# Attention and a gated layer on one core: more buffers for weight conversion, and loads and low parts moved in the order

## The chip, the cores and the metric

The kernel runs on one core of one Trainium2 chip. The metric is the device time of one launch in microseconds (us). The kernel before takes 1325.12 us, the median of three runs (1322.34 to 1326.35).

## The reference

```python
def _attn_ref(q, k, v):                       # 8 batches, 12 heads, 448 positions, head size 64
    S = q.shape[2]
    scores = q @ k.transpose(0, 1, 3, 2) / np.sqrt(q.shape[-1]) - np.log(S)
    return (1.0 / (1.0 + np.exp(-scores))) @ v          # a sigmoid in place of the softmax

def _moe_ref(x, w_gate, w_val, w_out):        # x 3584x768, w_gate and w_val 768x1536, w_out 1536x768
    gate = 1.0 / (1.0 + np.exp(-(x @ w_gate)))
    return gate * (x @ w_val) @ w_out
```

q, k and v come as float32. The attention's result, its heads side by side, is the x of the second part. The weights come as float64 and are read as pairs of 32-bit words. In the second part each operand is used as a high part and a low part, and three matmuls (low by high, high by low, high by high) make up one product.

## The kernel before

**Attention** (0 to about 279 us). The heads are taken in 24 groups of four ("quads", m = 0 to 23), three quads to a batch, and each quad in seven steps ("beats", g = 0 to 6). One beat has eight matmuls of `scores` (L254), a sigmoid on ScalarE (L266), and, two beats behind, the eight of `values` (L269). When a pair of heads is done, ScalarE copies one half of its sum out of PSUM and VectorE adds the other (`x<-av`, L297); the sum goes to DRAM (`xd`). There is one PSUM tile for each of the four sums of a quad, so TensorE can begin a sum of the next quad only when the add of the last one has been made, four beats earlier in the order.

**Conversion.** Beside this, VectorE and GpSimd turn the weights from float64 words into high and low parts. They come in chunks of 128x384. `Words.first` loads a chunk's next and does four VectorE operations (L109 to L112) on tiles `wa` and `wt`; `Words.second` does three more (L122 to L124), and `finish_lo` makes the low part (L128). `convert` (L130) is a generator that yields after each step. Each group of weights (one of six index pairs `jp`) has 32 steps. For each of two halves `t` there are four chunks of the gate or value weights, two steps each, with a cast and an add on GpSimd (L154, L157), and then four sums or differences of these chunks, one step each: an add and a cast on GpSimd (L167, L168) and the low part on VectorE (L170). These are the operands of a product with seven multiplications in place of eight. Then come four chunks of the output weights, two steps each, whose parts are sent to DRAM from `wa` and `wt` themselves (`od<-wt`, `od<-wa`, L139). The other results leave from tiles `whl` (three buffers) as `ad<-whl`. The first three groups (set 0) are converted in the attention at a fixed number of steps per beat, the other three (set 1) in the first visits of the second part, one step per 2.46 "ticks".

**x of the first batches.** From quad 8 on, `load_x` (L193) reads x of the first pair of batches back with 12 transfers, and `split_x` (L200), a generator too, makes of it seven operands of three tiles each in 21 steps: on GpSimd a difference (L209) and the cast to the high part (L213), on VectorE the low part (L215). One step is taken in beats 1, 3 and 5 of each quad from quad 9.

**The second part** has eight visits: set 0 with each of four pairs of batches (visits 0 to 3), then set 1 (visits 4 to 7). A visit has six units (gate and value, for each of three slots), and a unit has seven products of nine matmuls (`product`, L376), into four PSUM tiles `un`. ScalarE takes the first two products out of PSUM, VectorE the other five, in the order of the program, and GpSimd adds two of the partial sums (`u`, `c`, L393). A function in the list `later` is run after the matmuls of the next product. Each product also loads the operand that is seven ahead (`A<-ad`, L227); its transfer waits until TensorE has used the place. In a value unit, `value(i, acc)` multiplies gate and value (L438; VectorE for i = 0 and 2, GpSimd for 1 and 3), and `split` (L440) casts the result to its high part on ScalarE and takes the low part on VectorE.

Then come twelve output tiles of 18 matmuls each (L460). The first two take the first two slots before the last one. Eight places (`wo`) hold output weights: of the 18 loads of a visit eight have been made when its tiles begin, and three follow after every second tile (`load_out`, L231). In set 0 a tile is copied and stored as a partial sum (`part<-ob`). In set 1 the partial sum comes back (`pb<-part`, L466, two buffers), VectorE adds it (`plus`, L511), and the result is stored (`y<-ob`, two buffers of `ob`). Between the units and the tiles, x of the next visit is loaded, and its 21 split steps are taken two to a tile.

All transfers are issued by SyncE, in the order of the program. Each issue of the second part is also built to wait until the transfer eight issues before it has landed. VectorE, ScalarE and GpSimd run in the program's order too.

## Time and profile before

The profiled execution took 1328.51 us, of which the span from first to last instruction is 1326.7 us. It lies 3.4 us above the median of the runs.

| | TensorE | weight load | VectorE | ScalarE | GpSimd |
|---|---|---|---|---|---|
| busy, us | 1253.1 | 1029.1 | 757.0 | 440.4 | 483.2 |
| share of the span | 94% | 78% | 57% | 33% | 36% |

The granted TensorE clock was 0.983 on average. Transfers kept 78.5% of the 16 DMA engines' time, at 257 GB/s. In the rows, PE is TensorE, DVE VectorE, ACT ScalarE, POOL GpSimd and SPq the queue that issues transfers. A window's row gives its bounds and length in us, then each engine's busy time with the number of instructions, then the granted clock, the share of the DMA engines and GB/s. A row of waits gives the engine and line that waited, what it waited for, the us in total, the number of times and the longest. A row of the timeline gives start, length, instruction and, in brackets, the idle time before it with what ended it.

### The profile page before, as it was taken

The numbers are of one execution on the slowest core, as the hardware profiler recorded it, in microseconds if no ns is written. First come the engines' busy times: TensorE is split into PE (matmuls) and PEld (weight loads), VectorE is DVE, ScalarE is ACT, GpSimd is POOL, SyncE is SP. The second block draws the span as 40 slices with busy tenths as digits, with TensorE's granted clock in tenths as the row PEclk, the third lists the DMA queues.
The fourth block names the chain that finished last, engine by engine and source line by source line (L and its number), as shares of the span: only waits on it lengthen the run. The fifth ranks groups of instructions, "written<-read, shape, count | busy, mean of one in ns | idle before, by whom it ended". The sixth has DMA issues, their size and how long they took to land.

```text
span 1326.7 us, 20773 instructions
## 1 busy us (share of the span) xinstructions
PE 1253.1 (94%) x7456; PEld 1029.1 (78%) x7456; DVE 757.0 (57%) x1274; ACT 440.4 (33%) x700; POOL 483.2 (36%) x457
## 2 busy tenths in 40 slices
PE   9998789989998799978999899998999899989998
PEld 3443335768997799967899789997999799979998
DVE  6787888727757676645878645334434434443431
ACT  6776567732223122311242123222222312231210
POOL 3415824205563245612566233234123403241220
PEclk9999999999999899988999999999999999999999
DMA  8999688988978689676978876777777787778745
GB/s 316 319 349 326 241 274 311 317 281 253 312 263 303 200 271 334 218 278 198 308 271 294 281 241 214 217 216 251 242 216 213 232 263 217 230 227 269 215 128 178
DMA packets 159558, 341.12 MB, mean 257 GB/s; under 512 B 16352, under 2 KB 71776, under 8 KB 159456
## 3 DMA queue, kind: packets, MB, share of 16 engines
q1 hardware_dynamic: 159456, 339.80, 78.5%
q8 instruction: 59, 0.97, 0.3%
q14 instruction: 43, 0.35, 0.1%
HBM read 264.24 MB, written 75.50 MB: 256 GB/s over the span
## 4 chain that ended last, share of the span: by engine, by line
PE 61%; DVE 14%; DMA 11%; POOL 5%; issue 4%; SPq 2%; ACT 2%; DVEq 0%; POOLq 0%; ACTq 0%
PE un L385 34%; PE acc L460 14%; PE av L280 7%; PE sc L263 7%; DMA od<-wa 4%; DVE bl L215 2%; DMA wo<-od 2%; DVE c L393 1%; DMA ad<-whl 1%; DMA pb<-part 1%; DMA c<-xd 1%; POOL g L438 1%; DVE wa L109 1%; DVE wa L110 1%; DVE wt L122 1%
## 5 line engine op out<-in xcount | busy, mean ns | idle before, releaser
L385 PE MATMUL un<-bh,A 128*128 128x448 f32 x2016 | 590.1, 372 | 36.5 <-DVE c L393 19.3
L385 PEld LDWEIGHTS un<-bh,A 128*128 128x128 f32 x2016 | 385.2, 191 | 79.0 <-DVE c L393 23.8
L385 PE MATMUL un<-bl,A 128*128 128x448 f32 x1008 | 373.7, 371 | 0.0
L460 PE MATMUL acc<-hh,wo 128*128 128x448 f32 x1152 | 334.1, 369 | 15.0 <-DMA wo<-od 13.9
L460 PEld LDWEIGHTS acc<-hh,wo 128*128 128x128 f32 x1152 | 218.1, 189 | 36.9 <-DMA wo<-od 16.5
L280 PE MATMUL av<-a,v 64*64 64x448 f32 x1344 | 211.3, 540 | 16.0 <-DVE x L297 13.3
L460 PE MATMUL acc<-hl,wo 128*128 128x448 f32 x576 | 212.3, 369 | 0.5 <-DVE hl L442 0.4
L263 PE MATMUL sc<-qk 64*64 64x448 f32 x1344 | 211.0, 542 | 0.4 <-ACT a L266 0.4
L385 PEld LDWEIGHTS un<-bl,A 128*128 128x128 f32 x1008 | 192.5, 191 | 16.0
L266 ACT ACTIVATE a<-sc,bias 128x896 f32<-128x896 f32 x168 | 169.2, 1008 | 87.0 <-PE sc L263 77.2
L393 POOL TENSOR_TENSOR u<-u,p 128x448 f32<-128x448 f32 x48 | 56.1, 1169 | 388.8 <-DVE u L393 388.7
L441 ACT CAST hh<-g 128x448 fp32r<-128x448 f32 x96 | 52.8, 566 | 299.7 <-DVE g L438 232.0
L280 PEld LDWEIGHTS av<-a,v 64*64 64x64 f32 x1344 | 73.6, 134 | 78.8 <-issue 45.8
L263 PEld LDWEIGHTS sc<-qk 64*64 64x64 f32 x1344 | 73.1, 134 | 70.0 <-issue 52.2
L460 PEld LDWEIGHTS acc<-hl,wo 128*128 128x128 f32 x576 | 109.1, 189 | 10.4 <-DVE hl L442 1.4
L427 ACT ACTIVATE g<-c 128x448 f32<-128x448 f32 x96 | 51.6, 573 | 194.6 <-DVE c L393 191.8
L393 DVE TENSOR_TENSOR ob<-acc,pb 128x448 f32<-128x448 f32 x48 | 29.8, 622 | 121.4 <-DMA y<-ob 78.4
L442 DVE TENSOR_TENSOR hl<-g,hh 128x448 fp32r<-128x448 f32 x96 | 63.4, 663 | 62.0 <-ACT hh L441 61.4
L154 POOL CAST whl<-wt 128x384 fp32r<-128x384 f32 x48 | 37.5, 780 | 166.6 <-DVE wt L122 166.6
L438 POOL TENSOR_TENSOR g<-c,g 128x448 f32<-128x448 f32 x48 | 63.9, 1332 | 66.2 <-DVE c L393 63.6
L109 DVE TENSOR_SCALAR wa<-wraw 128x384 uint32<-128x384 uint32 x72 | 39.8, 552 | 80.2 <-DMA od<-wa 60.8
L393 DVE TENSOR_TENSOR c<-un,u 128x448 f32<-128x448 f32 x96 | 59.0, 618 | 31.2 <-PE un L385 29.8
(58 smaller groups left out, 1133.8 us busy)
## 6 DMA issues: line engine op xcount, KB each, us to landing
A<-ad SPq DMA_DIRECT2D x336, 384.0 KB, 3.9
wo<-od SPq DMA_DIRECT2D x144, 256.0 KB, 4.9
ad<-whl SPq DMA_DIRECT2D x84, 384.0 KB, 4.9
qk<-qk SPq DMA_DIRECT2D x23, 896.0 KB, 6.7
v<-vv SPq DMA_DIRECT2D x24, 448.0 KB, 6.3
xd<-x SPq DMA_DIRECT2D x48, 224.0 KB, 5.4
part<-ob SPq DMA_DIRECT2D x48, 224.0 KB, 4.2
pb<-part SPq DMA_DIRECT2D x48, 224.0 KB, 4.3
```

The source lines that it names most:

```text
L109: nc.vector.tensor_scalar(out=a, in0=raw[:, :, 1], scalar1=0x7FFFFFFF, scalar2=None, op0=ALU.bitwise_and)
L154: nc.gpsimd.tensor_copy(hl[:, 0], hi)
L263: nc.tensor.matmul(sc[halves[u], h, :S], lhsT=qkt[halves[h], p, k0:k0 + HP], rhs=qkt[halves[h], p, :S], start=True, stop=True)
L266: nc.scalar.activation(a, sc[:, :, :S], AF.Sigmoid, bias=bias, scale=scale)
L280: nc.tensor.matmul(avs[key][halves[h], :S], lhsT=vt[halves[u], g, h], rhs=a[halves[u], h], start=start, stop=g == last)
L385: nc.tensor.matmul(acc, lhsT=w, rhs=m, start=i == 0, stop=i == len(terms) - 1)
L393: engine.tensor_tensor(out=to, in0=x, in1=y, op=ALU.add)
L427: nc.scalar.activation(gates[i], acc, AF.Sigmoid)
L438: engine.tensor_tensor(out=g, in0=acc, in1=g, op=ALU.mult)
L441: nc.scalar.copy(hh, g)
L442: nc.vector.tensor_tensor(out=hl, in0=g, in1=hh, op=ALU.subtract)
L460: nc.tensor.matmul(acc, lhsT=w, rhs=m, start=i == 0 and some[0] == 0, stop=i == len(terms) - 1 and some[-1] == SET - 1)
```

## The change

- **Places.** In the attention `wa` and `wt` get four buffers in place of two and `whl` four in place of three. In the second part `wa` and `wt` get two in place of one; `whl` stays at three. `ob` gets three in place of two. A tile `wf4` is added, so that the second difference isn't written over the first sum.
- **Low parts of the sums** (`convert`). The VectorE operation of a sum, with its store, isn't issued at the start of the next step but goes to a list `unsplit`. There it waits until two sums stand behind it, or until a later step empties the list.
- **x of the first batches** is split in beats 1 and 5 of a quad, not 1, 3 and 5.
- **Low parts of the hidden values** (`value`). ScalarE's cast is issued at once where VectorE made the product and after the next product where GpSimd did. VectorE's low part follows one product behind the cast.
- **Loads.** The first two partial sums of a visit are loaded at its start, not between x and the tiles. `load_out` after every second tile stands ahead of that tile's add and of the next `pb` load.

```diff
@@ Words.first
-            a = self.pool.tile([P, CW], U32, tag="wa", name="wa")
-            t = self.pool.tile([P, CW], U32, tag="wt", name="wt")
+            a = self.pool.tile([P, CW], U32, tag="wa", name="wa", bufs=self.ahead)
+            t = self.pool.tile([P, CW], U32, tag="wt", name="wt", bufs=self.ahead)
@@ convert
+        def split(keep):
+            while len(unsplit) > keep:
+                to, hl, *where = unsplit.pop(0)
+                nc.vector.tensor_tensor(out=hl[:, 1], in0=to, in1=hl[:, 0], op=ALU.subtract)
+                store(hl, *where)
...
                     words.first()
+                    split(1)
                     send(1)
                     yield
                     send(0)
+                    split(0)
                     hi, a, e = words.second()
-                    hl = pool.tile([P, 2, CW], F32R, tag="whl", name="whl", bufs=3)
+                    hl = pool.tile([P, 2, CW], F32R, tag="whl", name="whl", bufs=words.held)
...
+                    split(1)
                     send(1)
-                    hl = pool.tile([P, 2, CW], F32R, tag="whl", name="whl", bufs=3)
+                    hl = pool.tile([P, 2, CW], F32R, tag="whl", name="whl", bufs=words.held)
                     nc.gpsimd.tensor_tensor(out=to, in0=x, in1=y, op=op)
                     nc.gpsimd.tensor_copy(hl[:, 0], to)
+                    unsplit.append((to, hl, jp, t, (1, 2, 3, 5)[n]))
                     yield
-                    nc.vector.tensor_tensor(out=hl[:, 1], in0=to, in1=hl[:, 0], op=ALU.subtract)
-                    store(hl, jp, t, (1, 2, 3, 5)[n])
@@
-        words = Words(att, chunks(sets[0]), AHEAD)
+        words = Words(att, chunks(sets[0]), AHEAD, 4)
...
-                if m > first_x and g % 2:
+                if m > first_x and g in (1, 5):
                     next(splits, None)
@@ value
-                def split():
+                def high():
                     nc.scalar.copy(hh, g)
-                    nc.vector.tensor_tensor(out=hl, in0=g, in1=hh, op=ALU.subtract)
-                if i == 2:
-                    split()
+                    later.append(lambda: nc.vector.tensor_tensor(out=hl, in0=g, in1=hh, op=ALU.subtract))
+                if engine is nc.vector:
+                    high()
                 else:
-                    later.append(split)
+                    later.append(high)
@@ visits
-        words = Words(ff, chunks(sets[1]), AHEAD_FF)
+        words = Words(ff, chunks(sets[1]), AHEAD_FF, 3)
...
             hs = []
+            if last_set:
+                load_part(pr, *tiles[0])
+                load_part(pr, *tiles[1])
...
                 load_x(nxt[1])
                 splits = split_x()
-            if last_set:
-                load_part(pr, *tiles[0])
-                load_part(pr, *tiles[1])
...
-                ob = ff.tile([P, S], F32, tag="ob", name="ob", bufs=2)
+                ob = ff.tile([P, S], F32, tag="ob", name="ob", bufs=3)
+                if t == 1:
+                    for _ in range(SET):
+                        load_out()
                 if s:
                     plus(ob, acc, pbs.pop((t, o)))
...
                 b = 2 * pr + t
-                if t == 1:
-                    for _ in range(SET):
-                        load_out()
```

How the order moves is shown at three places. In each the line numbers of the two kernels differ; the line of the same statement is 1 to 14 higher after, and L170 becomes L141.

SyncE between the units and the tiles of visit 5, before: the last load of x, three loads of partial sums, the first store, a fourth load, then the output weights.

```order
L197 DMA x_10463<-xd_5_94 128x448
L197 DMA x_10465<-xd_5_100 128x448
L466 DMA pb<-part_0_125 128x448
L466 DMA pb<-part_0_131 128x448
L466 DMA pb<-part_1_126 128x448
L522 DMA y<-ob 128x448
L466 DMA pb<-part_1_132 128x448
L235 DMA wo<-od_250 128x512
L235 DMA wo<-od_248 128x512
L235 DMA wo<-od_249 128x512
L522 DMA y<-ob 128x448
```

The same place after:

```order
L211 DMA x_10476<-xd_5_94 128x448
L211 DMA x_10478<-xd_5_100 128x448
L480 DMA pb<-part_1_126 128x448
L536 DMA y<-ob 128x448
L249 DMA wo<-od_250 128x512
L249 DMA wo<-od_248 128x512
L249 DMA wo<-od_249 128x512
L480 DMA pb<-part_1_132 128x448
L536 DMA y<-ob 128x448
```

The loads of `part_0_125` and `part_0_131` have gone to the visit's start, behind the last store of visit 4 and ahead of its first operand load. The three loads of output weights stand behind one load of a partial sum, not four.

VectorE in the last value unit of the last visit, before (L393 takes a product out of PSUM, L438 multiplies, L442 is the low part):

```order
L393 TENSOR_TENSOR c<-un,p_12375 128x448
L438 TENSOR_TENSOR g_12339<-c,g_12339 128x448
L442 TENSOR_TENSOR hl<-g_12339,hh 128x448
L393 TENSOR_TENSOR c<-un,u_12379 128x448
L442 TENSOR_TENSOR hl<-g_12354,hh 128x448
L442 TENSOR_TENSOR hl<-g_12357,hh 128x448
L393 TENSOR_TENSOR c<-un,u_12378 128x448
L438 TENSOR_TENSOR g_12373<-c,g_12373 128x448
L442 TENSOR_TENSOR hl<-g_12373,hh 128x448
```

The same after:

```order
L407 TENSOR_TENSOR c<-un,p_12391 128x448
L452 TENSOR_TENSOR g_12355<-c,g_12355 128x448
L456 TENSOR_TENSOR hl<-g_12355,hh 128x448
L407 TENSOR_TENSOR c<-un,u_12395 128x448
L407 TENSOR_TENSOR c<-un,u_12394 128x448
L452 TENSOR_TENSOR g_12389<-c,g_12389 128x448
L456 TENSOR_TENSOR hl<-g_12370,hh 128x448
L456 TENSOR_TENSOR hl<-g_12373,hh 128x448
L456 TENSOR_TENSOR hl<-g_12389,hh 128x448
```

The two low parts of what GpSimd multiplied have moved behind the last product's L407 and L452. ScalarE's and GpSimd's order in this place is unchanged.

VectorE in quads 9 and 10, where four sums are made (L170), x is split (L215) and the attention's sums are added (L297), before:

```order
L128 SCALAR_TENSOR_TENSOR whl<-wa,we 128x384
L215 TENSOR_TENSOR bl<-p_1298,bh 128x448
L170 TENSOR_TENSOR whl<-wf,whl 128x384
L297 TENSOR_TENSOR x<-av,x 128x448
L215 TENSOR_TENSOR bl<-u_1306,bh 128x448
L170 TENSOR_TENSOR whl<-wf,whl 128x384 x2
L297 TENSOR_TENSOR x<-av,x 128x448
L215 TENSOR_TENSOR bl<-g_1314,bh 128x448
L170 TENSOR_TENSOR whl<-wf,whl 128x384
L109 TENSOR_SCALAR wa<-wraw 128x384
```

The same after:

```order
L129 SCALAR_TENSOR_TENSOR whl<-wa,we 128x384
L311 TENSOR_TENSOR x<-av,x 128x448
L229 TENSOR_TENSOR bl<-p_1300,bh 128x448
L141 TENSOR_TENSOR whl<-wf,whl 128x384 x2
L311 TENSOR_TENSOR x<-av,x 128x448
L229 TENSOR_TENSOR bl<-u_1308,bh 128x448
L110 TENSOR_SCALAR wa<-wraw 128x384
L111 TENSOR_SCALAR wa<-wa 128x384
L112 TENSOR_SCALAR wt<-wa 128x384
L113 TENSOR_SCALAR wa<-wa 128x384
L141 TENSOR_TENSOR whl<-wf,whl 128x384 x2
```

The four low parts of the sums come later, the last two behind the first four operations of the next chunk, and two low parts of x stand where three stood.

13 lines of the change are left out of this document (9 added, 4 removed).

## The prediction

> **What bounds the kernel now.** I read the share of each engine on the page first, then busy times by stage, then in each slow stage what TensorE waits for, and then the queue behind that.
>
> ```profile
> PE 1253.1 (94%) x7456; PEld 1029.1 (78%) x7456; DVE 757.0 (57%) x1274; ACT 440.4 (33%) x700; POOL 483.2 (36%) x457
> ```
>
> TensorE is busy 94% of the span, so only what it loses can be won. The windows are cut where a stage's first matmul starts: the first nine quads; quads 9 to 16; then units and tiles of the visits.
>
> ```profile
> 4.46:98.80 94.34, 93.95 (x996) 38.04 (x992) 70.15 (x143) 69.91 (x80) 30.08 (x37) 1.00 0.96 335
> 98.80:203.30 104.50, 88.47 (x900) 35.96 (x896) 86.43 (x143) 62.76 (x72) 56.00 (x66) 0.98 0.80 279
> 279.30:365.20 85.90, 80.93 (x381) 72.78 (x380) 58.56 (x99) 17.96 (x35) 38.92 (x37) 0.96 0.87 287
> 365.20:409.50 44.30, 44.15 (x218) 40.48 (x217) 29.23 (x43) 17.13 (x34) 29.23 (x25) 1.00 0.77 266
> 409.50:504.00 94.50, 81.62 (x379) 72.97 (x378) 61.19 (x111) 17.27 (x34) 33.77 (x33) 0.95 0.81 260
> 548.50:647.50 99.00, 85.16 (x380) 75.24 (x379) 59.10 (x106) 19.25 (x38) 36.81 (x35) 0.91 0.73 245
> 692.40:775.00 82.60, 77.82 (x380) 70.70 (x380) 58.17 (x101) 18.54 (x36) 33.50 (x31) 1.00 0.85 280
> 775.00:821.80 46.80, 44.39 (x218) 40.50 (x217) 25.76 (x31) 17.29 (x34) 18.48 (x13) 1.00 0.70 225
> 821.80:898.40 76.60, 76.60 (x380) 70.98 (x379) 27.67 (x43) 18.50 (x35) 20.22 (x17) 1.00 0.76 217
> 898.40:948.50 50.10, 46.09 (x218) 41.81 (x217) 22.66 (x38) 11.94 (x23) 16.78 (x13) 0.97 0.72 231
> 1026.60:1077.30 50.70, 46.19 (x218) 41.79 (x217) 22.33 (x37) 11.95 (x23) 16.76 (x13) 0.97 0.72 225
> 1153.90:1202.40 48.50, 44.92 (x218) 40.23 (x217) 20.79 (x34) 11.95 (x23) 16.81 (x13) 1.00 0.73 231
> ```
>
> The kernel shows its own undisturbed pace: nine quads in 94.34 us (10.5 each), the units of visit 4 in 76.6 us (42 products, so 1.82 us each), the tiles of visit 0 in 44.3 us. Measured by these the losses are:
>
> - quads 9 to 16: 104.5 - 8 x 10.5 = 20.5 us
> - units of visits 1, 2 and 3: 94.5 + 99.0 + 82.6 - 3 x 76.6 = 46.3 us
> - tiles of visits 3 to 6: 46.8 + 50.1 + 50.7 + 48.5 - 4 x 44.3 = 18.9 us
> - units of visit 0: 85.9 - 76.6 = 9.3 us
>
> In visit 2 the loss of 22.4 us is 13.8 us of idle TensorE (99.0 - 85.16) and 9% of 99 us of clock that wasn't granted (8.9 us). A stall is paid for twice.
>
> **Term 1: second places for wa and wt.** The waits in visits 1 to 3 (409 to 775 us):
>
> ```profile
> DVE wa L109 <- DMA od<-wa: 52.5, 10, 9.3
> PE un L385 <- DVE c L393: 19.1, 8, 5.5
> PE un L385 <- DVE u L393: 12.1, 6, 4.2
> ```
>
> TensorE waits for VectorE to empty a PSUM tile, and VectorE stands at L109, the first operation of a chunk. One case, from both timelines:
>
> ```profile
> 412.22 0.56 DVE L128 SCALAR_TENSOR_TENSOR wa<-wa,we 128x384 fp32r<-128x384 uint32 x1
> 413.17 0.57 SPq L139 DMA_DIRECT2D od<-wa  x1
> 418.79 0.36 DVE L109 TENSOR_SCALAR wa<-wraw 128x384 uint32<-128x384 uint32 x1 [4.94 <-DMA od<-wa]
> 422.72 0.47 PE L385 MATMUL un<-bh,A 128*128 128x448 f32 x1 [1.68 <-DVE u L393]
> ```
>
> The store that empties `wa` is issued in the very step whose L109 needs it, since there is one `wa`. With two, L109 waits for the store of the chunk before last, issued one chunk earlier. A chunk is two steps of 2.46 ticks of 1.82 us, so that store has 9.0 us more. The longest wait was 9.3 us and the mean 5.25: nothing over 0.3 us is left if the store's path stays as it is. The load of the raw words stays ahead of the store as it was, and VectorE is busy 58 to 61 us of a visit's units, so the chunks fit. Bounds: 46 us if all is won, 23 if the waits are halved. I take **42**: ten waits gone, 4 us left for waits of another kind.
>
> **Term 2: quads 9 to 16.**
>
> ```profile
> PE av L280 <- DVE x L297: 13.3, 10, 2.3
> PE av L280 <- DMA v<-vv: 2.7, 1, 2.7
> DVE whl L170 <- POOL whl L168: 9.7, 6, 2.5
> L215 DVE TENSOR_TENSOR bl<-t,bh 128x448 fp32r<-128x448 f32 x6 | 5.9, 986 | 0.0
> L109 DVE TENSOR_SCALAR wa<-wraw 128x384 uint32<-128x384 uint32 x4 | 4.6, 1144 | 0.0
> L109 DVE TENSOR_SCALAR wa<-wraw 128x384 uint32<-128x384 uint32 x7 | 2.5, 361 | 4.3 <-DMA od<-wa 4.3
> ```
>
> The first three rows are of 98.8 to 203.3 us (the first two from 98), the next two of 122 to 150 us, the last of 60 to 98 us. TensorE waits because L297 comes late on VectorE, which is busy 86.4 of the 104.5 us: more than the 84.0 us that TensorE needs. Three things are taken off. At two steps a quad, 16 of the 21 steps of the split fall here, so five low parts of about 0.99 us move to quads 17 to 19: 4.9 us. The wait for GpSimd's cast goes, as the low parts are taken a step or two later: 9.7 us. One wait at L109 for an output-weight store (part of the remaining 8.4 us of idle VectorE) should go with four places. VectorE then needs 86.4 - 4.9 = 81.5 us and idles at most 8.4 more: 89.9 us; TensorE itself needs 84.0 and 2.7 for `v`, whose place behind the 12 loads of x doesn't change: 86.7 us. The load isn't even (chunks are denser than sums), so I take 92: a gain of **12.5**, bounds 4.9 (only the moved steps count) and 17.8.
>
> Against this term stand the two L109 rows: the same operation takes 361 ns in one stretch and 1144 ns in the other, where GpSimd subtracts for the split. VectorE's work grows when GpSimd's runs beside it, and low parts that no longer wait will run beside the next cast or subtraction.
> The Trainium skill's "SBUF — State Buffer", section "Who interferes with whom", has the rule: the two engines share one pair of ports, held for a whole instruction, and the second to issue is blocked until the first ends. The L109 rows agree. By it the 9.7 us of waiting for GpSimd would be turned into blocking, not won, and this term would be about 5 us in place of 12.5.
>
> **Term 3: loads at the visits' ends.** Visit 4, SyncE, VectorE and TensorE:
>
> ```profile
> 906.57 6.44 SPq L466 DMA_DIRECT2D pb<-part  x3
> g<-xd SPq DMA_DIRECT2D x4, 224.0 KB, 4.5
> 912.04 0.62 DVE L393 TENSOR_TENSOR ob<-acc,pb 128x448 f32<-128x448 f32 x1 [8.26 <-DMA pb<-part]
> 914.17 1.39 SPq L235 DMA_DIRECT2D wo<-od  x3
> 919.58 0.47 PE L460 MATMUL acc<-hh,wo 128*128 128x448 f32 x1 [4.01 <-DMA wo<-od]
> 920.65 0.57 PE L460 MATMUL acc<-hl,wo 128*128 128x448 f32 x1
> ```
>
> The third `pb` load needs the first one's place, so SyncE stands until the first add at 912.04; the ninth output weight is issued at 914.17, lands 5.4 us later, and TensorE has stopped at 915.58. After, the first two partial sums are there long before. SyncE leaves the x loads at 906.6 as now, issues one `pb`, one store and then the weights, at about 907.4; with the same 5.4 us they land at 912.8, 2.8 us before they are needed. The stall of 4.0 us goes, and the slow matmuls behind it (0.57 us at 920.65 where 0.36 is normal). Visits 4 to 6 lost 5.8, 6.4 and 4.2 us. Visit 3 has no partial sum to read: in its SyncE order nothing changes, and of its 2.5 us I count 1, since VectorE gets to its last chunk earlier. I take **16**; bounds 18.9, and 0 if the weights queue behind x's 12 x 224 KB = 2.7 MB.
>
> **What is added.** No arithmetic. VectorE no longer stands for a cast in the value units (the 18.3 us of L442 below), which wasn't TensorE's limit there, and `ob` with three places relieves an add that PSUM covers: nothing for both. At the end of a visit the low parts of the last unit come behind the next step of the conversion. The first two tiles begin with 24 matmuls of the first two slots, 24/9 x 1.82 = 4.9 us. In these VectorE must make the last multiply (0.88), up to four operations of the conversion (0.73 at most) and two or three low parts (0.68): 5.2 to 5.8 us. I count 0.5 us for each of visits 0 to 3, -2 us in all, bounds 0 and -4. The third item is GpSimd's:
>
> ```profile
> L442 DVE TENSOR_TENSOR hl<-g,hh 128x448 fp32r<-128x448 f32 x34 | 23.0, 680 | 18.3 <-ACT hh L441 18.3
> L438 DVE TENSOR_TENSOR g<-c,g 128x448 f32<-128x448 f32 x17 | 14.9, 877 | 0.6
> L123 DVE SCALAR_TENSOR_TENSOR wa<-wraw,wa 128x384 uint32<-128x384 uint32 x27 | 19.6, 726 | 0.0
> L168 POOL CAST whl<-wf 128x384 fp32r<-128x384 f32 x16 | 9.9, 618 | 1.7 <-DMA ad<-whl 0.8
> L167 POOL TENSOR_TENSOR wf<-wf 128x384 f32<-128x384 f32 x16 | 18.4, 1150 | 3.7 <-DVE whl L170 3.6
> ad<-whl SPq DMA_DIRECT2D x84, 384.0 KB, 4.9
> SPq L227 <- PE un L385: 407.5, 278, 8.7
> ```
>
> (All but the last two rows are of 409 to 775 us.) In the second part `whl` stays at three, while the stores go out later. The third and fourth sum need places whose stores are now issued in the same step. So GpSimd will wait at L168 for about 0.5 us of issue and 4.9 us of landing, less the 1.15 us of L167: 4.2 us, 12 times (six halves, two each). Behind it on GpSimd stand `u`, `c` and L438. The `u` made from the third product is needed with the sixth, three products on, and the sixth's PSUM tile is wanted again after three more: 3 x 1.82 = 5.5 us and as much again. The hold is covered; cost 0.
>
> **Sum.** 42 + 12.5 + 16 - 2 = 68.5 us. Against the profiled execution's 1328.5 us this gives 1260.0; the median lies 3.4 us under that execution, so 1257 us. Visit 0's 9.3 us stay.
>
> **Rivals.**
>
> *The waits at L109 are only shortened.* SyncE is in step with TensorE (its 407.5 us of waits for product places), so an issue can be late; then half of the 46 us stays: 1257 + 19 = 1276. Against it speaks that 9.0 us of lead meets waits of 5.25 on average. Chance 0.12.
> The Trainium skill's "TensorE: Matmul & The Clock Gate", section "What's actually happening", says that the clock is halved only after an idle window of about 3.4 us. The one stall of visit 3's tiles is about 2.4 us (46.80 - 44.39) and its clock 1.00, as the rule has it; by it halved stalls (5.5 becomes 2.7) would win back the whole clock, and this rival would end near 1269.
>
> *Output weights stay late,* behind x's transfers: term 3 is 0, 1273 us. For it: a landing of 5.4 us with the queue nearly empty; against: 2.8 us of room. Chance 0.10.
>
> *VectorE is the limit in quads 9 to 19 by itself:* term 2 is 5 us or less, 1265 us. Chance 0.14.
>
> *GpSimd's hold at L168 reaches TensorE: slower.* It happens at the 12 sums named above. Up to 11 us of hold the two covers of 5.5 us take it; beyond, each further us is TensorE's, with the clock on top. To eat the 68.5 us each hold must cost 5.7 us, so be near 17 us long, or 11 us with one cover missing. That gives 1330 us or more. The longest wait for a store in the rows above is 9.3 us; chance 0.03.
>
> *The change doesn't do what it says:* VectorE then waits at the same L109 for raw words instead, and times stay within 0.3% of 1325 (about what a measurement of this kernel tells from no change). The raw load is issued just ahead of the store and lands as early; chance 0.02.
>
> The forecast has 0.59. Its own range is 1247 to 1268. For 8 in 10 the upper end takes in the first three rivals and something of two together, 1283; the lower end, with all three terms at their best (46 + 17.8 + 18.9 = 82.7, so 1242), lies just under 1243. Faster by over 0.3%: 0.94; within: 0.03; slower: 0.03.
>
> **What would show it.** After, L109 should wait under 5 us for `od<-wa` in visits 1 to 3, and their units take 77 to 79 us. Quads 9 to 16 should take 90 to 95 us, with L170's successor waiting under 2 us for L168's. Tiles of visits 4 to 6 should take 44 to 45 us. GpSimd should show some 50 us of new waits for `ad<-whl` that nobody waits for. If the units of visits 1 to 3 still take over 85 us, term 1 is wrong; if TensorE waits for `u` or `c` with GpSimd at L168 ahead of it, the fourth rival is at work.

## The result and the profile after

The changed kernel takes 1256.69 us, the median of four runs (1252.40 to 1268.52), beside 1325.73 us for the kernel before (1322.34 to 1327.50). The ratio is 0.9496, 95% interval 0.9426 to 0.9567. The forecast was 1257 us. The profiled execution took 1259.75 us, its span is 1258.0 us, and the mean granted clock rose from 0.983 to 0.991. Of the kernel with the attention's part alone, below, no stage is read, since it was profiled in a launch of 2506.01 us where its nine others took 1317.88 to 1323.81 us.

The page's row of engines, after:

```profile
PE 1233.6 (98%) x7456; PEld 1014.1 (81%) x7456; DVE 775.1 (62%) x1274; ACT 440.0 (35%) x700; POOL 482.8 (38%) x457
```

TensorE is busy for 19.5 us less, though it does the same matmuls. About 11 us of that is granted clock won back (the part that was not granted is 1.7% of 1326.7 us before and 0.9% of 1258.0 us after); the slower pace that the last section describes is a part of the rest. What else was won came from idle time. The same stretches as before, cut again where a stage's first matmul starts: quads 9 to 16, units and tiles of visit 0, units of visits 1 and 2, tiles of visits 3 and 4.

```profile
99.10:198.40 99.30, 90.20 (x900) 37.11 (x896) 81.10 (x139) 62.51 (x72) 49.86 (x58) 0.93 0.88 301
276.40:359.80 83.40, 79.42 (x379) 72.78 (x380) 60.03 (x98) 17.59 (x35) 38.76 (x37) 0.96 0.89 294
359.80:407.20 47.40, 45.55 (x218) 41.78 (x217) 30.80 (x49) 17.31 (x34) 27.87 (x25) 0.96 0.81 275
407.20:483.80 76.60, 76.60 (x380) 70.97 (x379) 60.06 (x106) 17.54 (x34) 31.14 (x30) 1.00 0.92 300
528.70:608.10 79.40, 77.12 (x380) 70.82 (x379) 63.21 (x109) 19.05 (x38) 37.36 (x35) 1.00 0.91 306
728.90:772.70 43.80, 43.80 (x218) 40.59 (x217) 26.72 (x31) 17.20 (x34) 18.87 (x13) 1.00 0.75 243
849.30:893.10 43.80, 43.80 (x218) 40.60 (x217) 25.68 (x38) 11.87 (x23) 17.69 (x13) 1.00 0.87 287
```

From visit 3 on TensorE doesn't stop at all. Against the prediction's terms:

| stage | before, us | after, us | won | predicted |
|---|---|---|---|---|
| units of visits 1 to 3 | 276.1 | 232.6 | 43.5 | 42 |
| quads 9 to 16 | 104.5 | 99.3 | 5.2 | 12.5 |
| tiles of visits 3 to 6 | 196.1 | 175.2 | 20.9 | 16 |
| tiles of visits 0 to 2 | 133.7 | 136.5 | -2.8 | -2 (with visit 3) |
| units of visit 0 | 85.9 | 83.4 | 2.5 | 0 |
| units of visits 4 to 7 | 307.9 | 306.4 | 1.5 | 0 |
| quads 17 to 23 | 76.0 | 78.0 | -2.0 | 0 |

With 0.3 us lost in quads 0 to 8 these make 68.5 us; the spans differ by 68.7. The sum of the forecast (68.5) was met because a term that was too large and two that were too small cancelled, which is luck; so is a median within 1 us of the forecast, where the four runs lie 16 us apart.

What TensorE still waits for in the whole execution:

```profile
PE av L294 <- DVE x L311: 6.6, 2, 5.4
PE un L399 <- issue: 4.0, 1, 4.0
PE av L294 <- DMA v<-vv: 3.6, 1, 3.6
PE acc L474 <- DVE hl L456: 2.3, 3, 1.8
```

Before, the add of the attention's sums (L297, now L311) held TensorE ten times for at most 2.3 us; now it does so twice, and one of the two is 5.4 us long. The rows of the output weights (13.9 us in six waits in the whole execution before) and of VectorE's `u` and `c` are all but gone.

VectorE's and GpSimd's waits that the change was to move, the first two rows of 409 to 775 us, the last two of 276 to 775 us:

```profile
DVE wa L110 <- DMA od<-wa: 1.1, 1, 1.1
DVE hl L456 <- ACT hh L455: 6.4, 9, 2.3
...
POOL whl L180 <- DMA ad<-whl: 23.9, 10, 4.9
POOL whl L164 <- DMA ad<-whl: 8.3, 1, 8.3
```

The 52.5 us at the old L109 are 1.1 us; the 18.3 us for ScalarE's cast are 6.4; and GpSimd's hold is there, shorter and rarer than predicted.

### The profile page after: what moved, and what is told of

It reads as the page before. It is cut to its first block, busy times and chain, and to the rows that moved or that the text cites. A ratio compares the mean times of both kernels' runs of the same rounds, so it can differ in the third digit from the quotient of the medians.

```text
span 1258.0 us, 20754 instructions
## 1 busy us (share of the span) xinstructions
PE 1233.6 (98%) x7456; PEld 1014.1 (81%) x7456; DVE 775.1 (62%) x1274; ACT 440.0 (35%) x700; POOL 482.8 (38%) x457
## 4 chain that ended last, share of the span: by engine, by line
PE 88%; DVE 4%; DMA 3%; issue 1%; POOL 1%; SPq 1%; ACT 1%; POOLq 0%; ACTq 0%; DVEq 0%
PE un L399 47%; PE acc L474 26%; PE av L294 8%; PE sc L277 8%; DMA ad<-whl 1%; DMA p<-xd 1%; DMA v<-vv 0%; DVE hl L456 0%; DVE x L311 0%; POOL t L223 0%; DMA qk<-qk 0%; DVE wa L110 0%; DVE wa L111 0%; DMA wo<-od 0%; DVE c L407 0%
## 5 line engine op out<-in xcount | busy, mean ns | idle before, releaser
L399 PE MATMUL un<-bh,A 128*128 128x448 f32 x2016 | 576.5, 366 | 6.3 <-issue 4.0
L399 PEld LDWEIGHTS un<-bh,A 128*128 128x128 f32 x2016 | 379.9, 188 | 38.6 <-issue 5.0
L399 PE MATMUL un<-bl,A 128*128 128x448 f32 x1008 | 369.0, 366 | 0.0
L474 PE MATMUL acc<-hh,wo 128*128 128x448 f32 x1152 | 329.8, 366 | 0.3 <-ACT hh L455 0.3
L294 PE MATMUL av<-a,v 64*64 64x448 f32 x1344 | 207.1, 546 | 10.4 <-DVE x L311 6.6
L277 PE MATMUL sc<-qk 64*64 64x448 f32 x1344 | 207.2, 548 | 0.1
L399 PEld LDWEIGHTS un<-bl,A 128*128 128x128 f32 x1008 | 190.1, 189 | 14.9
L407 POOL TENSOR_TENSOR u<-u,p 128x448 f32<-128x448 f32 x48 | 56.0, 1167 | 368.4 <-DVE u L407 368.4
L474 PEld LDWEIGHTS acc<-hl,wo 128*128 128x128 f32 x576 | 108.6, 189 | 11.9 <-DVE hl L456 3.3
L407 DVE TENSOR_TENSOR u<-un,p 128x448 f32<-128x448 f32 x48 | 29.9, 623 | 119.7 <-PE un L399 119.6
L164 POOL CAST whl<-wt 128x384 fp32r<-128x384 f32 x48 | 37.9, 789 | 155.2 <-DVE wt L123 119.6
L407 DVE TENSOR_TENSOR c<-un,u 128x448 f32<-128x448 f32 x96 | 58.8, 621 | 38.2 <-PE un L399 31.7
L229 DVE TENSOR_TENSOR bl<-t,bh 128x448 fp32r<-128x448 f32 x72 | 62.3, 887 | 31.5 <-ACT bh L227 29.8
L407 DVE TENSOR_TENSOR ob<-acc,pb 128x448 f32<-128x448 f32 x48 | 29.9, 623 | 82.1 <-PE acc L474 72.3
L452 POOL TENSOR_TENSOR g<-c,g 128x448 f32<-128x448 f32 x48 | 57.5, 1200 | 52.1 <-DVE c L407 47.5
```

The source lines that it names most:

```text
L164: nc.gpsimd.tensor_copy(hl[:, 0], hi)
L229: nc.vector.tensor_tensor(out=lo, in0=x, in1=hi, op=ALU.subtract)
L277: nc.tensor.matmul(sc[halves[u], h, :S], lhsT=qkt[halves[h], p, k0:k0 + HP], rhs=qkt[halves[h], p, :S], start=True, stop=True)
L294: nc.tensor.matmul(avs[key][halves[h], :S], lhsT=vt[halves[u], g, h], rhs=a[halves[u], h], start=start, stop=g == last)
L399: nc.tensor.matmul(acc, lhsT=w, rhs=m, start=i == 0, stop=i == len(terms) - 1)
L407: engine.tensor_tensor(out=to, in0=x, in1=y, op=ALU.add)
```

## The experiments

Two kernels whose intervals overlap are compared by the stages in their traces; that is said each time.

### The three parts alone

**Places in the second part alone**, on the kernel before:

```diff
-            a = self.pool.tile([P, CW], U32, tag="wa", name="wa")
-            t = self.pool.tile([P, CW], U32, tag="wt", name="wt")
+            a = self.pool.tile([P, CW], U32, tag="wa", name="wa", bufs=2)
+            t = self.pool.tile([P, CW], U32, tag="wt", name="wt", bufs=2)
```

> The kernel before with one edit: in the second part wa and wt have two places in place of one (term 1 alone). Theory (the predicted term): the ten waits of L109 for od<-wa in visits 1 to 3 go, units of visits 1 to 3 fall from 276 us to about 234 us, the time falls by 42 us to about 1283 us; quads 9 to 16 and the tiles of visits 4 to 6 stay as they were. Rival (the waits are only halved, or only vanish together with the later low parts): 1300 us or more.

Measured: 1288.37 us against 1327.16, ratio 0.9715 (0.9670 to 0.9760), so 38.8 us. Units of visits 1 to 3 take 79.2, 78.2 and 76.6 us: 42.1 us less than before, the predicted 42. The waits of this kernel, VectorE's of 405 to 775 us, then TensorE's of the whole execution:

```profile
DVE hl L442 <- ACT hh L441: 20.6, 23, 1.6
DVE wa L109 <- DMA od<-wa: 1.2, 2, 0.8
...
PE acc L460 <- DMA wo<-od: 15.2, 5, 4.0
```

The mechanism of term 1 stands by itself, and the other two waits stay where they were: the 20 us of VectorE standing for ScalarE's cast can cost these units no more than the 4.2 us that they lie above 3 x 76.6, and the output weights are as late as before (tiles of visits 4 to 6: 49.9, 50.7, 49.5 us).

**Loads at the visits' ends alone**, on the kernel before (with the third place of `ob`):

```diff
             hs = []
+            if last_set:
+                load_part(pr, *tiles[0])
+                load_part(pr, *tiles[1])
...
-            if last_set:
-                load_part(pr, *tiles[0])
-                load_part(pr, *tiles[1])
...
+                if t == 1:
+                    for _ in range(SET):
+                        load_out()
                 if s:
...
-                if t == 1:
-                    for _ in range(SET):
-                        load_out()
```

> The kernel before with the loads of the visits' ends alone: the first two partial sums at the visit's start, output weights ahead of the add, three places for ob. Theory: tiles of visits 4 to 6 fall from about 49.8 to 44 us each, in all 16 us, so about 1309 us; tiles of visit 3 nearly unchanged, since nothing in their order moves. Rival (the changed kernel won there because VectorE came earlier, not because of the loads): under 6 us, over 1319 us.

Measured: 1307.56 us, ratio 0.9852 (0.9813 to 0.9891), so 19.6 us. Tiles of visits 4, 5 and 6 take 43.8 us each. Visit 3's stay slow (48.2), with the one wait for output weights that is left between 700 and 1220 us:

```profile
PE acc L460 <- DMA wo<-od: 2.6, 1, 2.6
```

So term 3 was right for visits 4 to 6, and visit 3's loss is not the loads' affair. What cures it is found below.

**The attention's part alone** (four places each, later low parts of the sums, split in two beats), the second part as before:

```diff
-        words = Words(att, chunks(sets[0]), AHEAD)
+        words = Words(att, chunks(sets[0]), AHEAD, 4, 4, True)
...
-                if m > first_x and g % 2:
+                if m > first_x and g in (1, 5):
...
-        words = Words(ff, chunks(sets[1]), AHEAD_FF)
+        words = Words(ff, chunks(sets[1]), AHEAD_FF, 3, 1, False)
```

(The numbers are the places of `whl` and of `wa` and `wt`; the last argument says whether the sums' low parts wait.)

> The attention's part of the change alone: four places for wa and wt, four for whl, low parts of the sums later, x split in beats 1 and 5; the second part as before. Predicted term: 12.5 us, so about 1313 us. What the changed kernel's profile suggests instead: quads 9 to 16 give 5 us back and no more, about 1320 us, with one long stall of TensorE near quad 14 and a longer one for v at quad 9.

Measured: 1318.96 us, ratio 0.9944 (0.9919 to 0.9969), so 8.2 us (4 to 11). The 12.5 us of term 2 would be 0.9906, just outside the interval; 5 us would be 0.9962, inside. The two stalls that were expected can't be looked for in this kernel.

### Why quads 9 to 16 won less than 12.5 us

In the changed kernel six of the eight quads run at 10.5 to 10.8 us, the undisturbed pace. All that is left is in two: quad 9 takes 17.2 us (`v` late by 3.6 us) and quad 14 takes 18.7. Before, seven of the eight took 12.1 to 15.0 us. Of the 20.5 us of loss 15.3 are left, nearly all of it in two quads. In quad 14 TensorE stops at 163.34 us until VectorE's L311 ends at 168.71. GpSimd's timeline and then VectorE's, of that time:

```profile
158.15 1.24 POOL L223 TENSOR_TENSOR t<-x,t 128x448 f32<-128x448 f32 x1
159.46 0.57 POOL L227 CAST bh<-t 128x448 fp32r<-128x448 f32 x1
...
162.24 1.44 POOL L223 TENSOR_TENSOR c<-g,c 128x448 f32<-128x448 f32 x1
...
166.48 0.69 POOL L227 CAST bh<-u 128x448 fp32r<-128x448 f32 x1
```
```profile
159.53 2.32 DVE L141 TENSOR_TENSOR whl<-wf,whl 128x384 fp32r<-128x384 f32 x2
161.78 0.91 DVE L123 SCALAR_TENSOR_TENSOR wt<-wraw,wt 128x384 uint32<-128x384 uint32 x1
162.61 1.49 DVE L124 SCALAR_TENSOR_TENSOR wa<-wraw,wa 128x384 uint32<-128x384 uint32 x1
...
168.09 0.62 DVE L311 TENSOR_TENSOR x<-av,x 128x448 f32<-128x448 f32 x1
169.15 0.55 DVE L123 SCALAR_TENSOR_TENSOR wt<-wraw,wt 128x384 uint32<-128x384 uint32 x1
169.62 0.55 DVE L124 SCALAR_TENSOR_TENSOR wa<-wraw,wa 128x384 uint32<-128x384 uint32 x1
```

VectorE is busy for 11.49 of the 11.70 us from 157.0 on; its operations are long. L123 and L124 take 0.91 and 1.49 us while GpSimd is at work, and 0.55 each right after it has stopped. The chunks of the output weights have come up, for which GpSimd has no work of its own, so it runs ahead through the split's steps one behind the other.

**Without GpSimd's twelve differences** in the split of the first batches; this kernel leaves these subtractions out, so four of the seven operands of x of the first pair of batches are x itself, and what follows from them is not the reference's:

```diff
-    def split_x(cast=nc.scalar.copy):
+    def split_x(cast=nc.scalar.copy, diff=True):
...
-                if n in (1, 2, 3, 6):
+                if not diff and n == 1:
+                    xs[4, k] = xs[0, k]
+                if diff and n in (1, 2, 3, 6):
...
-                    splits = split_x(nc.gpsimd.tensor_copy)
+                    splits = split_x(nc.gpsimd.tensor_copy, False)
```

> The changed kernel without GpSimd's 12 differences in the split of x of the first pair of batches (the operands are made from x itself; the result for these batches is not the reference's). If the stall at quad 14 comes from VectorE's operations growing while GpSimd works beside them, L110 to L113 in 150 to 170 us shrink (mean of L110 from over 0.8 to about 0.5 us) and the stall of 5.4 us goes or falls under 2 us. If it comes from the low parts of two sums standing in the next chunk's steps, the stall stays above 3 us.

Measured: 1243.58 us, ratio 0.9364 (0.9328 to 0.9401), wholly below the changed kernel's interval. Quads 10 to 22 all run at 10.52 us, quad 14 too. The means of two VectorE operations around quad 14 by the groups of lines, first of this kernel (142 to 164 us), then of the changed kernel (148 to 170 us):

```profile
L141 DVE TENSOR_TENSOR whl<-wf,whl 128x384 fp32r<-128x384 f32 x4 | 3.5, 926 | 0.0
L110 DVE TENSOR_SCALAR wa<-wraw 128x384 uint32<-128x384 uint32 x4 | 1.8, 446 | 0.0
```
```profile
L141 DVE TENSOR_TENSOR whl<-wf,whl 128x384 fp32r<-128x384 f32 x4 | 5.1, 1306 | 0.8 <-POOL whl L180 0.8
L110 DVE TENSOR_SCALAR wa<-wraw 128x384 uint32<-128x384 uint32 x2 | 1.4, 683 | 0.0
```

With the differences gone VectorE's operations shorten by a third and the stop disappears: it was GpSimd's operations beside VectorE's that made it.

**The sums' low parts at once in the attention**, as before the change; the rival cause, that they land together with the chunks:

```diff
+                    if not words.defer:
+                        split(0)
...
-                    split(1)
+                    split(1 if words.defer else 0)
...
-        words = Words(att, chunks(sets[0]), AHEAD, 4)
+        words = Words(att, chunks(sets[0]), AHEAD, 4, 4, False)
```

> The changed kernel with the low parts of the sums taken at once, as before, in the attention only (later in the second part as in the change). If the later low parts cause the stall at quad 14, quad 14 falls from 18.6 to under 13 us; VectorE then waits for GpSimd's cast again, some 10 us over quads 9 to 16, and the time is within 5 us of the changed kernel's. If they are what won, quads 9 to 16 take 104 us again and the time is 5 us or more above.

Measured: 1255.33 us, ratio 0.9465 (0.9413 to 0.9518), not told apart from the changed kernel by time. By the stage: quad 14 still takes 17.4 us with a stop of 5.1. The order of the sums' low parts is not the cause. Nor is it what won. This kernel's quads 9 to 16 and VectorE's longest wait in them:

```profile
99.10:192.10 93.00, 86.31 (x896) 37.21 (x892) 80.58 (x139) 62.47 (x72) 50.38 (x58) 0.98 0.89 317
```
```profile
DVE whl L141 <- POOL whl L182: 7.5, 3, 3.2
```

VectorE waits for GpSimd's cast for 7.5 us, near the 9.7 of before, and yet these quads take 93.0 us, no more than with the later low parts. The rest of the attention's part, the four places and the two split steps a quad, won what was won; these two were not separated.

**The split taken apart**: GpSimd makes only the difference, ScalarE the cast a step later, VectorE the low part a step after that:

```diff
+    def split_x_apart():
+        casts, lows = [], []
+        def behind():
+            if lows:
+                x, hi, lo = lows.pop(0)
+                nc.vector.tensor_tensor(out=lo, in0=x, in1=hi, op=ALU.subtract)
+            if casts:
+                x, hi, lo = casts.pop(0)
+                nc.scalar.copy(hi, x)
+                lows.append((x, hi, lo))
...
+                behind()
...
+                casts.append((x, hi, lo))
+                yield
...
-                    splits = split_x(nc.gpsimd.tensor_copy)
+                    splits = split_x_apart()
```

> The changed kernel with the split of x in the attention taken apart: ScalarE makes the casts to the high part, a step after GpSimd's difference, and VectorE the low part a step after that. The result is the reference's. Theory (VectorE's operations grow while GpSimd works beside them): GpSimd's 21 casts are gone from beside VectorE's conversion, so the stall at quad 14 (17 to 18.6 us in all versions that keep GpSimd's casts and differences) shrinks by half or more, to under 14 us, and the time falls by 4 to 7 us. Rival (only the differences matter, two inputs each): quad 14 stays over 16 us. Risk: ScalarE's sigmoids behind a late cast, which would show as stalls of TensorE's values in quads 10 to 20.

Measured: 1246.78 us, ratio 0.9392 (0.9365 to 0.9420), below the changed kernel's interval. Quad 14 takes 14.5 us, just over the 14 that was expected, and its stop 2.0. Half of quad 14's loss (8.1 us, now 4.0) went when the casts left GpSimd; that the low part also comes a step later was not tested alone.

**`v` ahead of x**: the twelve loads of x begin at beat 2 of their quad, behind the load of the next `v`:

```diff
-                if m == first_x and g == 0:
+                if m == first_x and g == LAG:
```

> The changed kernel with the 12 loads of x at quad 8 two beats later, so that the load of v for quad 9 stands ahead of them. Theory: the stall of TensorE at quad 9 (17.2 us in place of 10.5 in the changed kernel's profile) is the load of v behind the loads of x, and it passes the length at which the clock is lowered; without it quad 9 takes 10.5 to 11 us, the time falls by about 6 us to 1250. Rival: v would be late anyway, since the engines' queue is full: no gain.

Measured: 1254.17 us, ratio 0.9440 (0.9412 to 0.9467), not told apart by time. By the stage: TensorE doesn't wait for `v` any more, but 0.9 us for the next `qk`, and quad 9 takes 11.6 us, not 17.2; quad 14 stays at 17.6. The 5.6 us are what it won against this one trace. The wait for `v` differs from execution to execution, as the table shows. The rows with four places and with the old order are kernels described further below, whose attention is the changed kernel's line for line. Each time is from the first `scores` matmul of a quad to that of another:

| kernel | quad 9, us | its stop, us | quad 14, us | quads 9 to 16, us |
|---|---|---|---|---|
| before | 13.5 | 2.7 for `v` | 12.9 | 104.5 |
| changed | 17.2 | 3.6 for `v` | 18.7 | 99.3 |
| four places for `whl` | 12.6 | 1.8 for `v` | 17.5 | 94.0 |
| old order of low parts | 11.9 | 1.1 for `v` | 18.5 | 95.0 |
| old order, four places | 15.1 | 2.7 for `v` | 18.1 | 96.6 |
| sums at once | 12.1 | 1.3 for `v` | 17.4 | 93.1 |
| `v` first | 11.6 | 0.9 for `qk` | 17.6 | 92.7 |
| split taken apart | 14.1 | 3.4 for `v` | 14.5 | 92.2 |
| without differences | 12.0 | 1.3 for `v` | 10.5 | 85.7 |

The 5.2 us that quads 9 to 16 won are so the least of four executions of the same attention; the others won 7.9 to 10.5. Quad 14's loss is there in each of them.

### What GpSimd's hold and the low parts' order cost

**Four places for `whl`** in the second part (with two for `ob`, for room):

```diff
-        words = Words(ff, chunks(sets[1]), AHEAD_FF, 3)
+        words = Words(ff, chunks(sets[1]), AHEAD_FF, 4)
...
-                ob = ff.tile([P, S], F32, tag="ob", name="ob", bufs=3)
+                ob = ff.tile([P, S], F32, tag="ob", name="ob", bufs=2)
```

> The changed kernel with four places for whl in the second part (and two for ob, to make room). The waits of GpSimd at the cast of the sums for ad<-whl (23.9 us in the changed kernel's second part) fall under 8 us. If nobody waits for them, as predicted, the time is the changed kernel's within 3 us; if they reach TensorE, it is 5 us or more below.

Measured: 1251.13 us, ratio 0.9422 (0.9398 to 0.9446), which just overlaps the changed kernel's interval. GpSimd's waits at L180 for `ad<-whl` fall from 23.9 to 2.9 us, as expected. By the stages, units of visit 2 take 77.4 us in place of 79.4, tiles of visit 1 43.8 in place of 44.9: 3 us, the price of the hold.

**The hidden values' low parts in the order of before**, all else as changed:

```diff
-                def high():
+                def split():
                     nc.scalar.copy(hh, g)
-                    later.append(lambda: nc.vector.tensor_tensor(out=hl, in0=g, in1=hh, op=ALU.subtract))
-                if engine is nc.vector:
-                    high()
+                    nc.vector.tensor_tensor(out=hl, in0=g, in1=hh, op=ALU.subtract)
+                if i == 2:
+                    split()
                 else:
-                    later.append(high)
+                    later.append(split)
```

> The changed kernel with the low parts of the hidden values taken as before. If the later low parts are what costs the 3 us at the end of visit 0 (TensorE waits there for VectorE's low part, which stands behind a step of the conversion), tiles of visit 0 fall from 47.4 to about 44.3 us and the time is 1 to 4 us under the changed kernel's. If they also spare VectorE stalls that TensorE would feel in the units, units of visits 1 to 3 grow by some us and the time is above the changed kernel's.

Measured: 1273.04 us, ratio 0.9583 (0.9520 to 0.9645): 16 us above the changed kernel, where by the prediction's terms it should have been at or a little below it. The two intervals overlap by their ends, but the fastest runs of the two lie 15 us apart as well, and by the stages units and tiles of visits 1 to 3 take 14.1 us more. Tiles of visit 1 take 49.1 us, of visit 3 48.4. The chain behind visit 1's stop, by the timelines of GpSimd, ScalarE, VectorE and TensorE:

```profile
483.08 0.50 POOL L180 CAST whl<-wf 128x384 fp32r<-128x384 f32 x1 [1.16 <-DMA ad<-whl]
483.54 2.27 POOL L452 TENSOR_TENSOR g<-c,g 128x448 f32<-128x448 f32 x2
484.73 0.57 ACT L455 CAST hh<-g 128x448 fp32r<-128x448 f32 x1 [5.36 <-POOL g L452]
485.32 0.97 DVE L456 TENSOR_TENSOR hl<-g,hh 128x448 fp32r<-128x448 f32 x1 [3.76 <-ACT hh L455]
487.95 0.61 DVE L407 TENSOR_TENSOR c<-un,u 128x448 f32<-128x448 f32 x1
489.88 0.63 PE L474 MATMUL acc<-hh,wo 128*128 128x448 f32 x1 [3.14 <-ACT hh L455]
```

GpSimd holds for a store, its multiply is late, ScalarE's cast waits for that, VectorE stands for the cast with the last product's `c` queued behind it, and TensorE waits for what comes of that `c`. In the changed kernel GpSimd holds at the same place longer (2.44 and 0.57 us), but VectorE has `c` ahead of the low parts and TensorE stops for 0.3 us.

**The same with four places for `whl`**, to take that hold out from under the old order:

```diff
-        words = Words(ff, chunks(sets[1]), AHEAD_FF, 3)
+        words = Words(ff, chunks(sets[1]), AHEAD_FF, 4)
...
-                    later.append(lambda: nc.vector.tensor_tensor(out=hl, in0=g, in1=hh, op=ALU.subtract))
+                    nc.vector.tensor_tensor(out=hl, in0=g, in1=hh, op=ALU.subtract)
...
-                    later.append(high)
+                    later.append(split)
...
-                ob = ff.tile([P, S], F32, tag="ob", name="ob", bufs=3)
+                ob = ff.tile([P, S], F32, tag="ob", name="ob", bufs=2)
```

> The changed kernel with the low parts of the hidden values in the order of before, and with four places for whl (two for ob) in the second part. In the run with the old order alone, TensorE's stop of 3.14 us in visit 1's tiles (at 486.7 us) was led back to GpSimd: its waits at L180 for a store of whl (1.40 and 1.16 us) delay the multiplication L452, ScalarE's cast waits 5.36 us for it, VectorE waits 3.76 us for the cast, with the last sum c and the last multiplication queued behind that. Theory (GpSimd's hold on whl is what the old order of the low parts can't stand): without the hold visit 1's units and tiles fall from 79.6 and 49.1 to 77 to 78 and 44 to 46 us, visit 2's from 80.5 and 44.9 to 77 to 78 and 44 to 45, no stop over 1 us is left there; about 1260 us where the rest of the kernel runs at the pace of 202.7 ns a matmul, 1267 where it runs at 206.7 ns. Rival (the old order costs by itself, through ScalarE's and VectorE's order around the last unit): visit 1's tiles stay above 48 us with a stop at their beginning, and the time stays at 1270 to 1277 us.

Measured: 1261.43 us, ratio 0.9511 (0.9480 to 0.9542). Tiles of visit 1 fall from 49.1 to 45.0 us and the stop is gone: that stop was the hold. But the time is still 10 us above four places with the new order (0.9422, intervals apart): units of visits 1 and 2 take 79.2 and 79.5 us, not 77 to 78 as expected, and visit 3's tiles 48.0; units and tiles of visits 1 to 3 take 11.2 us more together. The last is the stop that the loads alone hadn't cured. VectorE, SyncE and TensorE around it, old order with four places:

```profile
732.54 0.63 DVE L456 TENSOR_TENSOR hl<-g,hh 128x448 fp32r<-128x448 f32 x1 [0.63 <-ACT hh L455]
733.08 0.55 DVE L123 SCALAR_TENSOR_TENSOR wt<-wraw,wt 128x384 uint32<-128x384 uint32 x1
733.66 0.37 SPq L147 DMA_DIRECT2D od<-wt  x1
742.78 1.52 SPq L249 DMA_DIRECT2D wo<-od  x3
747.47 0.74 PE L474 MATMUL acc<-hh,wo 128*128 128x448 f32 x1 [2.06 <-DMA wo<-od]
```

And the same three lines with the new order and four places, where TensorE doesn't stop:

```profile
720.99 0.55 DVE L123 SCALAR_TENSOR_TENSOR wt<-wraw,wt 128x384 uint32<-128x384 uint32 x1
721.57 0.37 SPq L147 DMA_DIRECT2D od<-wt  x1
730.32 1.81 SPq L249 DMA_DIRECT2D wo<-od  x3
```

The tiles begin at 727.9 us in the one and 719.2 us in the other, so the conversion step comes 5.2 us after that in the old order and 1.8 us in the new. Its store stands on SyncE ahead of all loads of x and of the output weights: these are issued 14.9 and 11.1 us after the tiles' beginning. The later low parts help by letting the conversion step, and so SyncE, go first.

### Together

**Four changes at once**: `v` first, four places for `whl` (again with two for `ob`), the conversion of visit 0 begun nine products later, and the list `later` emptied once more in the last unit:

```diff
-                if m == first_x and g == 0:
+                if m == first_x and g == LAG:
...
+                if slot == SET - 1 and i == 2:
+                    run_later()
...
-        words = Words(ff, chunks(sets[1]), AHEAD_FF, 3)
-        ... convert(words, sets[1]), 32 * SET, [0], [0], 66 * B // 2 - 28
+        words = Words(ff, chunks(sets[1]), AHEAD_FF, 4)
+        ... convert(words, sets[1]), 32 * SET, [0], [-9], 66 * B // 2 - 37
```

> The changed kernel with four places for whl in the second part (two for ob), v ahead of x at quad 8, the conversion in visit 0 begun nine products later, and the low parts of a visit's last slot taken ahead of the next conversion step. By stage: quad 9 under 12 us; units of visit 0 from 83.4 to 77 to 78 us, if the stall there is VectorE waiting for the raw words of set 1; tiles of visit 0 from 45.4 to 47.4 to about 44.3 us, if the low parts behind a conversion step are what they wait for. In all about 1241 to 1244 us. Rival for visit 0: the raw words are late by more than nine products, or the stall moves to the next step: units stay above 81 us.

Measured: 1249.71 us, ratio 0.9413 (0.9369 to 0.9458), no better than four places for `whl` alone. Visit 0's units fall from 83.4 to 78.5 us; with `v` first alone or four places alone they had stayed at 84.1 and 84.3, so by elimination the conversion beside its first products was most of their loss (4.9 of 6.8 us). Its tiles take 48.1 us, not the 44.3 expected, and tiles of visits 2 and 3 lose 1.0 and 1.7 us against 43.8, in visit 3 for output weights. Which of the last two edits gives this back was not separated.

**The same with the split taken apart** as above:

```diff
-                    splits = split_x(nc.gpsimd.tensor_copy)
+                    splits = split_x_apart()
```

> The two kernels before together: about 1235 to 1239 us, quads 9 to 22 nearly all at 10.5 us, and no stall of TensorE over 2 us but the one at the start of the second part, if any.

Measured: 1242.40 us (1241.16 to 1244.14), ratio 0.9357 (0.9333 to 0.9381). It beats both kernels: the one before by 6.4%, the changed one by 14 us of medians, with the intervals of the two ratios apart. It lies 3 us above the upper end of what was expected. Up to its last matmul TensorE is idle for 9 us, and no wait is over 2.0 us; the longest:

```profile
PE av L325 <- DVE x L342: 2.0, 1, 2.0
```

## Why the prediction was right, and where it wasn't

**What bounds the kernel, and how a loss is priced: right.** The loss by stage against the kernel's own undisturbed pace was what could be won: 68.7 us of the 95 counted.

**Term 1, right: 43.5 us for 42.** With the places alone the units won 42.1 us, and the wait at L109 fell from 52.5 to 1.2 us. The rival of halved waits has fallen, by both traces.

**Term 2, mis-sized: 5.2 us for 12.5, and 7.9 to 10.5 in three other executions of the same attention.** The sum was "VectorE then needs 86.4 - 4.9 = 81.5 us and idles at most 8.4 more". VectorE does need 81.1 us. The step that failed is that the 9.7 us of waiting for GpSimd's cast are taken off as a gain. The wait did shrink as said (1.3 us), but with the low parts at once it is 7.5 us and the quads are as fast. What these quads still lose is nearly all in quads 9 and 14.

Quad 14 costs 7.0 to 8.1 us. I spread VectorE's work over the eight quads with an allowance of 2 us for unevenness, and it comes in one lump of some ten operations, many two to three times as long as usual (L124 at 1.49 us beside 0.55). The run without the differences shows that GpSimd's operations make the lump's stop; that a shared pair of ports is the way is not shown. The rule of the Trainium skill's "SBUF — State Buffer", section "Who interferes with whom", by which the waiting would turn into blocking, fits the long operations in quad 14 (1.49 us beside 0.55). But VectorE's busy time didn't grow by the 9.7 us (81.1 us where 81.5 was predicted without any blocking), so that the 5 us worked out from the rule lies near 5.2 is chance.

Quad 9 lost 6.7 us (`v` behind the loads of x), and 1.4 to 4.6 us in the other three; 2.7 us had been counted, and that a stop can cost a lower clock as well was left out. Quads 17 to 23 take 2.0 us more than before, with a stop of 1.2 us for L311 in quad 20; the steps of the split that were moved there had been counted at nothing.

**Term 3, mechanism right, 20.9 us for 16.** Two things were missed. The tiles' undisturbed length was taken as 44.3 us from visit 0, where it is 43.8; four times this difference is what lies beyond the upper bound of 18.9. And visit 3, counted at 1 us since "in its SyncE order nothing changes", won 3.0: SyncE's order is the same there, but it stands at a store whose data VectorE makes 3.4 us sooner (5.2 against 1.8 us) with the new order of low parts.

**Later low parts, "nothing" and 0.5 us a visit: wrong in both directions.** The cost shows in visit 0's tiles alone, 3.1 us in the changed kernel (TensorE waits 1.85 us for L456 there, and the clock drops); it differs from kernel to kernel, 45.4 us with four places and 48.1 with the split taken apart, beside 44.9 and 45.7 with the old order. The gain, costed at nothing, is the larger: with the old order the kernel is 16 us slower by medians, 10 us where GpSimd doesn't hold; by the stages of visits 1 to 3 it is 14.1 and 11.2 us. What was overlooked is the queue behind the standing instruction: on VectorE the last `c` and the conversion step stand behind a low part that waits for a cast, and behind the conversion's store stands all of SyncE. Against 76.6 us for units and 43.8 for tiles, visits 1 to 3 lose 51.1 us before, 10.1 with the places alone, 18.4 with the whole change but the old order, 12.4 with four places for `whl` as well, 4.3 in the changed kernel and 1.2 with four places and the new order. So a loss of the old order's size is there already with the places alone, where 42 us were won in spite of it. That the waits at L109 hid it before is likely, but not shown.

**GpSimd's hold, "covered; cost 0": about 3 us.** It waits at L180 ten times for 23.9 us, and 8.3 us once at L164, where some 50 us were predicted. No TensorE wait names it, but a fourth place takes 2.0 us from visit 2's units and 1.1 from visit 1's tiles, and 6.0 us from visits 1 to 3 with the old order. The fourth rival's mechanism exists, far from the 5.7 us a hold that it needed.

**Visit 0's 9.3 us** stayed mostly, 6.8 us; the run with the later conversion points to the conversion beside its first products for most of it.

## What to carry to other kernels

A wait of a busy engine is not a gain because it is long: leave it in while the rest is changed, and see whether the stage gets slower. When the limit in a stage is an engine's share of a lump of work, spread neither its load nor its waits over the stage: look for the densest stretch, and price operations there by their length beside the other engine's work, not by their mean. Where an in-order engine waits for another engine's result, cost the wait by everything queued behind it, on that engine and on the queue whose next transfer needs its data; a wait that costs nothing while a slower one covers it can cost once the slower one is removed. A place more for a store's source is worth its room where the store is issued in the step that needs the place.

## What the runs showed of the hardware

**Two paces of the matmuls at full granted clock.** Visit 5's units and tiles in the kernel with `v` first, then in the changed kernel:

```profile
889.90:968.00 78.10, 78.10 (x380) 70.94 (x379) 28.64 (x44) 18.02 (x34) 19.60 (x17) 1.00 0.73 220
968.00:1012.60 44.60, 44.60 (x217) 40.52 (x216) 24.40 (x38) 11.86 (x23) 17.59 (x13) 1.00 0.84 279
```
```profile
893.10:969.70 76.60, 76.60 (x380) 71.00 (x379) 28.86 (x44) 18.00 (x34) 19.57 (x17) 1.00 0.79 223
969.70:1013.50 43.80, 43.80 (x218) 40.60 (x217) 26.20 (x38) 11.97 (x23) 18.07 (x13) 1.00 0.87 286
```

TensorE is busy without a stop in all four, the clock reads 1.00, and the same 378 and 216 matmuls take 1.5 and 0.8 us more: 206.7 against 202.7 ns each. In the traces here a pace holds until something delays a matmul: it changed at stops, and in visit 3 of both kernels with the old order at a single matmul that started 235 ns after the one before (at about 712 and 707 us). The changed kernel keeps the pace that it has after its last stop (614.1 us) for 3158 matmuls; at 4 ns each the other pace would cost it 12.6 us. This would explain why kernels with few stops left have runs in two groups some 10 us apart. With the old low parts these are 1267.28 and 1268.23, 1277.85 and 1279.22 us, and the profiled one (1277.85) ran at the slow pace from visit 4 on. The profiled executions of the kernels with `v` first (1264.01 us, the others 1252.20 to 1254.54) and with the sums at once (1266.94, the others 1250.61 to 1255.51) did so from visit 3 on. Of the other runs no pace is known. A part of the 16 us above is then pace; the 10 us don't rest on it, since both profiled executions there ran at the fast pace from visit 4 on and differ by 13 us. What picks the pace isn't known.

**The clock after a stop doesn't go by the stop's length alone.** After a stop of 1.85 us in the changed kernel (from 365.56 us), and after one of 3.38 us in the kernel with the split taken apart (from 102.69 us):

```profile
367.56:369.56 2.00, 2.00 (x8) 1.82 (x9) 0.41 (x1) 1.44 (x3) 0.93 (x1) 0.70 1.05 370
369.56:371.56 2.00, 2.00 (x7) 1.80 (x6) 0.75 (x2) 0.57 (x3) 1.61 (x1) 0.50 0.99 348
```
```profile
104.69:106.69 2.00, 0.62 (x8) 0.36 (x12) 0.78 (x2) 0.00 (x0) 1.00 (x2) 1.00 1.02 403
106.69:108.69 2.00, 2.00 (x24) 0.77 (x20) 0.00 (x0) 0.76 (x1) 1.91 (x3) 1.00 1.06 424
```

The clock that isn't granted, added up over such rows from the start of the stop (one less the clock, times 2 us), is 1.7 us for the short stop, half the clock for 3.4 us, and nothing for the long one. For the stops of 3.60 and 5.42 us in the changed kernel's quads 9 and 14 it is 3.4 us each. In the traces here it is 0, 1.7 or 3.4 us after every stop of over 1 us that has no other near it; the shortest that cost clock is one of 1.73 us (loads alone, from 126.09 us), the longest that cost none is the one of 3.38. The prediction's reading, by which only an idle window of about 3.4 us lowers the clock, does not fit. That a stop counts by how it falls into windows that run free of the kernel would fit these rows; it was not tested.
